# An attention, channel MLP and expert attention kernel: one operand's copies on another queue, early sums read out by another engine, and a new table of tile modes

## The chip, the cores and the metric

The kernel runs on one core of a Trainium2 chip. The metric is the device time of one execution in microseconds (us), a median over runs. The core has five instruction streams: TensorE (PE; its weight loads are shown apart as PEld), VectorE (DVE), ScalarE (ACT), GpSimd (POOL) and SyncE (SP), which here only issues transfers. Each stream runs its instructions in order; semaphores tie them together. Sums of TensorE stand in PSUM, everything else in SBUF.

## The reference

Three blocks follow one another on arrays of 2 batches, 768 positions and 512 columns. The first is an attention of 8 heads of width 64, in which a query sees only keys whose six projection signs equal its own; the second is a position mixer of rank 32 with a channel MLP; the third is four causal attentions, of which each position takes the best two by a gate.

```python
# 1: per head, S = 768, D = 64
mask = bucket(q @ proj)[:, None] == bucket(k @ proj)[None, :]
attn = softmax(where(mask, q @ k.T / 8, -1e9)) @ v
# 2: x is attn with the heads side by side (512 columns)
u = x + (x.T @ U @ V).T
x = u + relu(u @ w_ch1) @ w_ch2          # 512 -> 2048 -> 512
# 3: four experts, causal, width 64, best two by the gate
out = sum(gate_e * softmax(causal(x @ wq_e @ (x @ wk_e).T / 8)) @ (x @ wv_e) @ wo_e)
```

## The kernel before

The results need more than half precision, so nearly every operand is held as a high and a low half in float16, and a product takes two or three matmuls (high with high, high with low, low with high).

**First block (a1).** The work is 8 pairs of heads, four to a batch: (0,0) to (0,3), then (1,0) to (1,3). A head has 6 tiles of 128 queries by 768 keys, so a pair has 12 tiles and the block 96. For a tile TensorE makes the scores `sc` (L621, L626), VectorE reduces them (`L632`, which also moves them to SBUF as P32), ScalarE takes the exponent (L543 or L591). What follows goes by the tile's mode, from the table `A1_MODES`, which is run through again and again over a pair's 12 tiles. A mode of two letters names who makes the high half (L545 on ScalarE for A, L547 on VectorE for V) and who subtracts it to get the low half (L551, on GpSimd for P or VectorE for V); both halves are then turned by a transfer (`dma_start_transpose`, L643), and 18 matmuls of 64 columns (L555 to L557) multiply them with the values. A mode that begins with F keeps float32: TensorE transposes (L597), ScalarE or VectorE reads the result out (L602, L604, by the mode's second and third letter), and float32 matmuls (L606) multiply with the values, without a transfer.

**Operands of a pair** (`a1_prep`) are made one pair ahead. The queries' high half HQ lies in a staging tile TQ and goes by transfer into AQ and a second time into BQ (L454); so do the keys' halves into AK and BK (L461 to L463). The program's names carry buffer numbers; BQ and BK have two buffers, used by turns. The first pair has a path of its own (`a1_first`), in which `BQE1` makes the second copy.

**Weights.** The MLP's two matrices arrive as 64-bit floats, in 32 units of 128 by 512 words. A unit is a transfer into w or wx (L277), three integer operations on VectorE (L189, L192, L195) that make float32, a copy to float16 on ScalarE (L280) and a scaling and a subtraction on GpSimd (L281, L282). When units are asked for is set by counts: NWA0 over the first PRE0 tiles, NWA and NW1 over the next ones, and then NWB plus WRATE per step of the MLP (`need`).

**MLP.** Six tiles of the first product are summed early, over the first two quarters of the columns (`early`, L322), and moved by `EVICT` to the tiles acc. The first 512 positions go through `mlp_wide`: ph (L748, twelve matmuls of 512 columns a tile) is read out by L755 on ScalarE and L756 on VectorE, and px (L770) by L773 on VectorE. The other blocks go through `mlp_stream` (ph L806, px L824). `merge` weaves a1 and the MLP together by costs: MIX says how many a1 tiles are spread over how much MLP.

**Order.** The order above is only a wish. A list scheduler with a timeline of its own places each engine's instructions by priority (the order of writing, shifted by `sooner`, `AHEAD` and the like) and by when it expects operands and buffers to be free. So a changed count or mode moves instructions elsewhere too.

Of the kernel before, what the change touches and what calls it, by code (L numbers as in the profile page):

```python
# [15 lines left out]
AF = mybir.ActivationFunctionType  # L16
# [6 lines left out]
def kernel(  # L23
# [17 lines left out]
    nc = tc.nc  # L41
# [19 lines left out]
    CLIP = 8e9  # L61
    WPOOL = True
    A1_MODES = (
        [('AP', 'FAA'), ('FAV', 'AP', 'FAV'), ('AP', 'VP', 'FAV', 'AP', 'VP', 'AP', 'FAV', 'AP', 'VP', 'AP', 'FAV', 'FAV'), ('AP', 'FAA', 'VP', 'FAV')],
        [('AP', 'VP'), ('AP', 'AP', 'AV'), ('AP', 'AV', 'VP'), ('AP', 'AP', 'AV')],
    )
    A2_MODES = ("AP", "AP")
    MIX = (24, 2.2)
    LAST_MODES = ("PV", "AP", "PV", "T")
    VPOS = 1  # L70
    FPOS = 3
    BQE1 = lambda o, i: nc.scalar.activation(o, i, AF.Copy)
    KLE = nc.gpsimd
    KLE0 = (nc.vector, nc.gpsimd)
    SKE = lambda o, k, a: nc.scalar.activation(o, k, AF.Copy, scale=-0.125)
# [8 lines left out]
    PJ = nc.vector  # L84
    AHEAD = 80
    AHEAD2 = 150
    AHEAD3 = 300
    N4 = 7
    W4 = 1.0
    SOON = 20  # L90
# [3 lines left out]
    FIRST = 2  # L94
    SSE = lambda s: nc.scalar.activation(s, s, AF.Copy, bias=0.25e-9, scale=0.25)
    PRE1 = 48
    PRE0 = 42
    EVICT = nc.vector.tensor_copy
    XNB = 1
    LAGS = (2, 4, 4)  # L100
    LAST_LAGS = (1, 1, 1)
# [102 lines left out]
    VV = cp.tile([4 * R, S], FH, name="VV")  # L204
# [205 lines left out]
    HALF = (slice(0, D), slice(D, P))  # L410
# [19 lines left out]
    def q_halves(j, qn, AQ, BQ):  # L430
# [3 lines left out]
        nc.vector.scalar_tensor_tensor(lo, hi, 8.0, qn, op0=ALU.mult, op1=ALU.add)  # L434
        BQE1(BQ[HALF[0], j], hi)

# [6 lines left out]
    def a1_prep(b, p, wait):  # L443
        qn, kn, vn = nats.pop((b, p))
        n = f"{b}_{p}"
        AQ, AK, BQ, BK, V = a1_operands(b, p)
        TQ = sp.tile([P, 2, S], FH, tag="TQ", name=f"TQ_{n}")
        HQ, LQ = TQ[:, 0], TQ[:, 1]
        nc.scalar.activation(HQ, qn, AF.Copy, scale=-0.125)
        nc.vector.scalar_tensor_tensor(LQ, HQ, 8.0, qn, op0=ALU.mult, op1=ALU.add)  # L450
        for j, o in enumerate(HALF):
            nc.sync.dma_start(AQ[HALF[0], j], HQ[o])
            nc.sync.dma_start(AQ[HALF[1], j], LQ[o])
            nc.sync.dma_start(BQ[HALF[0], j], HQ[o])  # L454
        TK = sp.tile([P, 3, S], FH, tag="TK", name=f"TK_{n}")
        HK, SK, LK = TK[:, 0], TK[:, 1], TK[:, 2]
        nc.scalar.activation(HK, kn, AF.Copy)
# [676 lines left out]
    def merge(*a):  # L1134
        drain(merged(*a))
# [46 lines left out]
                yield from a2_stream(b, s0 // P, (s0 + n) // P)  # L1182

    NWA0 = 8
    NWA = 5
    NW1 = 16
    NWB = 18
    WRATE = 0.8

# [36 lines left out]

    merge(take(a1, PRE0), PRE0 * CA, w_stream(NWA0), NWA0)
    C = (PRE1 - PRE0) * CA
    merge(take(a1, PRE1 - PRE0), C, merged(w_stream(NWA), NWA - NWA0, early_stream(), NPRE), NPRE + NWA - NWA0)
    merge(take(a1, PH1 - PRE1), (PH1 - PRE1) * CA, w_stream(NW1), NW1 - NWA)  # L1230
    C = MIX[1] * UNIT
    merge(take(a1, MIX[0]), CA * MIX[0], part(mlp, C), C)
    C = LEAD[0] * UNIT
    merge(a1, CA * (NA1 - PH1 - MIX[0]), part(mlp, C), C)
    C = LEAD[1] * UNIT
# [13 lines left out]
    merge(take(g4, N4), N4, part(mlp, C), C)  # L1249
    ahead[0] = AHEAD3  # L1250
    drain(mlp)
# [59 lines left out]
```

## Time and profile before

| | |
|---|---|
| median of 3 runs | 606.88 us (603.32 to 608.47) |
| profiled execution, its own time | 604.46 us |
| span of its instructions | 602.7 us |
| mean granted TensorE clock | 0.984 |

The span is what the profile's rows cover; about 1.8 us of the execution's time lies outside it. A busy TensorE in a row is not TensorE at its peak: the end of a matmul is modelled, so matmuls that follow one another with gaps may still fill their stretch. The pace of matmuls that are packed shows in the chain of work, where each is counted from its start to the next one's start. In the names of rows a number at the end of a tile's name is left out (P is P32, x_0_0 an MLP sum).

### The profile page before, as it was taken

To read this page: it belongs to the slowest core of one execution; us is meant where nothing else is said; L and a number is where in the kernel's file an instruction comes from. 1 tells how busy PE (TensorE), PEld (TensorE's weight loads), DVE (VectorE), ACT (ScalarE), POOL (GpSimd) and SP (SyncE) were. 2 spreads that over 40 slices of the span, in tenths; PEclk is the share of its full clock that TensorE was granted. 3 is DMA by queue.
4 is the path that set the end of the run, shared out by engine and by line. 5 is a ranking of instruction groups with operands and counts; after the bars stand their busy time and mean duration, and the time that the engine had idled before them with its cause. 6 is when DMAs were issued, how large, how long until landed. Compare 5 with 4: busy or idle time off the path is not lost.

```text
span 602.7 us, 14989 instructions
## 1 busy us (share of the span) xinstructions
PE 555.8 (92%) x5982; PEld 416.1 (69%) x5982; DVE 412.1 (68%) x948; ACT 351.9 (58%) x753; POOL 260.3 (43%) x239
## 2 busy tenths in 40 slices
PE   3789996899899999799999989999999998999995
PEld 1468864776555545447888866878877898999754
DVE  6976897759999999858768455553564335455584
ACT  6798787767564665645768534672465216144683
POOL 6644579745967698622246400250134002002350
PEclk9889999999899999999999999999999999999998
DMA  8789899989999999782479910153046002004655
GB/s 268 170 174 179 225 209 263 187 216 216 316 190 208 237 216 240 159 197 63 92 133 141 177 25 10 36 94 92 4 86 125 36 1 46 12 18 41 121 106 114
DMA packets 176566, 82.00 MB, mean 136 GB/s; under 512 B 160368, under 2 KB 167152, under 8 KB 176496
## 3 DMA queue, kind: packets, MB, share of 16 engines
q1 hardware_dynamic: 176496, 81.04, 62.2%
q8 instruction: 47, 0.77, 0.6%
q14 instruction: 23, 0.19, 0.1%
HBM read 29.30 MB, written 3.15 MB: 54 GB/s over the span
## 4 chain that ended last, share of the span: by engine, by line
PE 59%; DVE 16%; DMA 11%; issue 5%; ACT 5%; POOL 2%; SPq 1%; DVEq 0%; ACTq 0%; POOLq 0%
PE px L824 12%; PE ph L806 11%; DMA PT<-HL 6%; PE px L770 3%; PE po L606 3%; DVE P L632 2%; PE pk L875 2%; PE pq L875 2%; PE sc L621 2%; PE sc L626 2%; PE pv L903 2%; PE ph L748 2%; PE pz L1106 2%; PE s L974 2%; DMA wx<-in_moe_w_ch_dram 2%
## 5 line engine op out<-in xcount | busy, mean ns | idle before, releaser
L551 POOL TENSOR_TENSOR HL<-P,HL 128x768 f16<-128x768 f32 (+5 forms) x91 | 121.3, 1338 | 258.4 <-ACT HL L545 197.2
L543 ACT ACTIVATE P<-P,m 128x768 f32<-128x768 f32 (+5 forms) x110 | 89.4, 813 | 40.7 <-DVE P L632 26.2
L806 PE MATMUL ph<-U,W 128*128 128x256 f16 (+1 forms) x960 | 95.4, 251 | 0.5 <-DVE hT L808 0.5
L824 PE MATMUL px<-hT,W 128*128 128x256 f16 (+1 forms) x960 | 94.1, 251 | 0.0
L824 PEld LDWEIGHTS <-W 128*128 128x128 f16 x960 | 78.2, 98 | 8.4
L806 PEld LDWEIGHTS <-W 128*128 128x128 f16 x960 | 77.0, 98 | 8.7 <-issue 0.8
L632 DVE TENSOR_SCALAR_CACHE_REDUCE P<-sc 128x768 f32<-128x768 f32 x80 | 74.9, 947 | 11.0 <-PE sc L626 10.9
L545 ACT ACTIVATE HL<-P 128x768 f16<-128x768 f32 (+5 forms) x91 | 63.1, 696 | 9.7 <-DMA PT<-HL 8.5
L555 PEld LDWEIGHTS <-PT 128*128 128x128 f16 x522 | 47.6, 98 | 16.8 <-DMA PT<-HL 8.3
L621 PE MATMUL sc<-AK,AQ 128*128 128x512 f16 x192 | 49.0, 335 | 6.2 <-DVE P L632 2.7
L556 PEld LDWEIGHTS <-PT 128*128 128x128 f16 x522 | 47.4, 98 | 5.4 <-issue 1.9
L555 PE MATMUL po<-V,PT 128*128 128x64 f16 x378 | 43.5, 193 | 6.6 <-DMA PT<-HL 3.2
L626 PE MATMUL sc<-BK,BQ 96*128 96x512 f16 x192 | 49.6, 336 | 0.0
L557 PEld LDWEIGHTS <-PT 128*128 128x128 f16 x522 | 47.5, 98 | 1.7 <-issue 0.2
L770 PE MATMUL px<-hT,W 128*128 128x512 f16 x192 | 44.4, 379 | 0.8 <-DVE acc L754 0.4
L808 DVE SCALAR_TENSOR_TENSOR hT<-ph,hT 128x256 f16<-128x256 f32 (+1 forms) x80 | 28.8, 366 | 23.1 <-ACT hT L807 22.3
L557 PE MATMUL po<-V,PT 128*128 128x64 f16 x378 | 44.2, 193 | 0.0
L556 PE MATMUL po<-V,PT 128*128 128x64 f16 x378 | 44.2, 193 | 0.0
L807 ACT ACTIVATE hT<-ph 128x256 f16<-128x256 f32 (+1 forms) x80 | 26.4, 334 | 28.9 <-PE ph L806 28.0
L748 PE MATMUL ph<-U,W 128*128 128x512 f16 x156 | 36.3, 380 | 1.7 <-DVE hT L756 1.3
L982 DVE TENSOR_SCALAR_CACHE_REDUCE P<-s 128x128 f32<-128x128 f32 (+5 forms) x48 | 29.3, 620 | 9.1 <-PE s L979 8.0
L770 PEld LDWEIGHTS <-W 128*128 128x128 f16 x192 | 18.1, 98 | 20.6 <-DVE acc L754 0.8
(257 smaller groups left out, 1252.1 us busy)
## 6 DMA issues: line engine op xcount, KB each, us to landing
w<-in_moe_w_ch_dram SPq DMA_DIRECT2D x17, 512.0 KB, 5.1
wx<-in_moe_w_ch_dram SPq DMA_DIRECT2D x15, 512.0 KB, 5.6
vn<-in_v_dram SPq DMA_DIRECT2D x8, 384.0 KB, 4.5
out_dram<-o SPq DMA_DIRECT2D x12, 256.0 KB, 2.1
kn<-in_k_dram SPq DMA_DIRECT2D x7, 384.0 KB, 4.6
qn<-in_q_dram SPq DMA_DIRECT2D x7, 384.0 KB, 4.0
AK<-TK SPq DMA_DIRECT2D x28, 96.0 KB, 2.7
AQ<-TQ SPq DMA_DIRECT2D x28, 96.0 KB, 3.1
```

The source lines that it names most:

```text
L543: nc.scalar.activation(P32, P32, AF.Exp, bias=m, scale=-1.0, accum_out=ssum)
L545: nc.scalar.activation(HL[:, 0], P32, AF.Copy)
L551: eng.tensor_tensor(HL[:, 1], P32, HL[:, 0], op=ALU.subtract)
L555: nc.tensor.matmul(o, PT[:, t, :], vh(t), start=(t == 0), stop=False)
L556: nc.tensor.matmul(o, PT[:, t, :], vl(t), start=False, stop=False)
L557: nc.tensor.matmul(o, PT[:, nk + t, :], vh(t), start=False, stop=(t == nk - 1))
L621: nc.tensor.matmul(ps[:, c0 : c0 + cn], aq[:, P * t : P * (t + 1)], ak[:, c0 : c0 + cn], start=True, stop=False,)
L626: nc.tensor.matmul(ps[:, c0 : c0 + cn], bq[:, P * t : P * (t + 1)], bk[:, c0 : c0 + cn], start=False, stop=True,)
L632: nc.vector.tensor_scalar(P32, ps[:, 0:S], CLIP, None, op0=ALU.min, op1=ALU.min, accum_out=m)
L770: nc.tensor.matmul(po, w, u, start=(i == 0), stop=(i == len(ops) - 1))
L806: nc.tensor.matmul(ph, w, u, start=(i == 0), stop=(i == len(ops) - 1))
L824: nc.tensor.matmul(po, w, u, start=(i == 0), stop=(i == len(ops) - 1))
```

## The change

It does five things. (1) HQ's second copies for pairs 2 to 8 (L454, 14 transfers of 64 by 768) are issued by ScalarE instead of SyncE; in the first pair the second copy, made by two ScalarE copies (L72), becomes two transfers on SyncE (L435). (2) The six early sums are read out by ScalarE (L98) instead of VectorE (L323). (3) Counts: PRE0 42 to 44, NWA 5 to 6, NW1 16 to 9, so that by the order of writing fewer weight units are asked for ahead of the MLP. (4) Modes: pair (0,3) goes from 3 AP, 3 VP, 6 F to 3 AP, 1 AV, 1 VV, 7 F. Of batch 1's 48 tiles, those that subtract on VectorE (AV) go from 12 to 2, AP from 26 to 35, VP from 10 to 11: pair (1,0) from 6 AP, 6 VP to 8 and 4; (1,1) from 8 AP, 4 AV to 12 AP; (1,2) from 4 AP, 4 AV, 4 VP to 9 AP, 3 VP; (1,3) from 8 AP, 4 AV to 6 AP, 4 VP, 2 AV. (5) MIX from 24 to 26 tiles, and AHEAD3 from 300 to 200.

```diff
--- before.py
+++ after.py
@@ -61,15 +61,15 @@
     CLIP = 8e9
     WPOOL = True
     A1_MODES = (
-        [('AP', 'FAA'), ('FAV', 'AP', 'FAV'), ('AP', 'VP', 'FAV', 'AP', 'VP', 'AP', 'FAV', 'AP', 'VP', 'AP', 'FAV', 'FAV'), ('AP', 'FAA', 'VP', 'FAV')],
-        [('AP', 'VP'), ('AP', 'AP', 'AV'), ('AP', 'AV', 'VP'), ('AP', 'AP', 'AV')],
+        [('AP', 'FAA'), ('FAV', 'AP', 'FAV'), ('AP', 'VP', 'FAV', 'AP', 'VP', 'AP', 'FAV', 'AP', 'VP', 'AP', 'FAV', 'FAV'), ('AV', 'FAV', 'FAV', 'AP', 'VV', 'FAA', 'FAA', 'FAV', 'AP', 'FAV', 'AP', 'FAV')],
+        [('VP', 'AP', 'VP', 'AP', 'VP', 'AP', 'AP', 'AP', 'VP', 'AP', 'AP', 'AP'), ('AP',), ('AP', 'VP', 'AP', 'AP'), ('AP', 'VP', 'VP', 'AV', 'AP', 'AP')],
     )
     A2_MODES = ("AP", "AP")
-    MIX = (24, 2.2)
+    MIX = (26, 2.2)
     LAST_MODES = ("PV", "AP", "PV", "T")
     VPOS = 1
     FPOS = 3
-    BQE1 = lambda o, i: nc.scalar.activation(o, i, AF.Copy)
+    BQE1 = nc.sync.dma_start
     KLE = nc.gpsimd
     KLE0 = (nc.vector, nc.gpsimd)
     SKE = lambda o, k, a: nc.scalar.activation(o, k, AF.Copy, scale=-0.125)
@@ -84,7 +84,7 @@
     PJ = nc.vector
     AHEAD = 80
     AHEAD2 = 150
-    AHEAD3 = 300
+    AHEAD3 = 200
     N4 = 7
     W4 = 1.0
     SOON = 20
@@ -94,8 +94,8 @@
     FIRST = 2
     SSE = lambda s: nc.scalar.activation(s, s, AF.Copy, bias=0.25e-9, scale=0.25)
     PRE1 = 48
-    PRE0 = 42
-    EVICT = nc.vector.tensor_copy
+    PRE0 = 44
+    EVICT = lambda o, i: nc.scalar.activation(o, i, AF.Copy)
     XNB = 1
     LAGS = (2, 4, 4)
     LAST_LAGS = (1, 1, 1)
@@ -451,7 +451,7 @@
         for j, o in enumerate(HALF):
             nc.sync.dma_start(AQ[HALF[0], j], HQ[o])
             nc.sync.dma_start(AQ[HALF[1], j], LQ[o])
-            nc.sync.dma_start(BQ[HALF[0], j], HQ[o])
+            nc.scalar.dma_start(BQ[HALF[0], j], HQ[o])
         TK = sp.tile([P, 3, S], FH, tag="TK", name=f"TK_{n}")
         HK, SK, LK = TK[:, 0], TK[:, 1], TK[:, 2]
         nc.scalar.activation(HK, kn, AF.Copy)
@@ -1182,8 +1182,8 @@
                 yield from a2_stream(b, s0 // P, (s0 + n) // P)
 
     NWA0 = 8
-    NWA = 5
-    NW1 = 16
+    NWA = 6
+    NW1 = 9
     NWB = 18
     WRATE = 0.8
```

The scheduler then moves much. The first place is VectorE in the second head of pair (1,1); the first list is before, the second now (w are weight units, U and xn the mixer's, x_0_0 and hT the MLP's).

```order
L632 TENSOR_SCALAR P_1_1_1_2_3525,m_1_1_2_3524<-sc_1_1_2_3519 128x768
L189 TENSOR_SCALAR w_14_x<-w_14_64_3061 128x512
L192 SCALAR_TENSOR_TENSOR w_14_x<-w_14_64_3061,w_14_x 128x512
L195 SCALAR_TENSOR_TENSOR w_14_32_3062<-w_14_64_3061,w_14_x 128x512
L551 TENSOR_TENSOR HL_1_1_2_3527<-P_1_1_1_2_3525,HL_1_1_2_3527 128x768
L189 TENSOR_SCALAR w_15_x<-w_15_64_3125 128x512
L652 TENSOR_TENSOR xn_1_3018<-po_1_0_3019,r_1_0_3405 128x6x64
L632 TENSOR_SCALAR P_1_1_1_3_3582,m_1_1_3_3581<-sc_1_1_3_3576 128x768
L192 SCALAR_TENSOR_TENSOR w_15_x<-w_15_64_3125,w_15_x 128x512
L208 SCALAR_TENSOR_TENSOR U_1_3119<-up_0_3608,U_0_3118 128x768
L195 SCALAR_TENSOR_TENSOR w_15_32_3126<-w_15_64_3125,w_15_x 128x512
L632 TENSOR_SCALAR P_1_1_1_4_3657,m_1_1_4_3656<-sc_1_1_4_3651 128x768
```

In the changed kernel the same place reads:

```order
L632 TENSOR_SCALAR P_1_1_1_2_3497,m_1_1_2_3496<-sc_1_1_2_3491 128x768
L208 SCALAR_TENSOR_TENSOR knw<-wqs,qnw 128x1024
L773 SCALAR_TENSOR_TENSOR x_0_0_2293<-px_0_2_0_3224,x_0_0_2293 128x512
L632 TENSOR_SCALAR P_1_1_1_3_3544,m_1_1_3_3543<-sc_1_1_3_3538 128x768
L652 TENSOR_TENSOR xn_1_2998<-po_1_0_2999,r_1_0_3378 128x6x64
L756 SCALAR_TENSOR_TENSOR hT_0_2292<-ph_0_3_0_3421,hT_0_2292 128x512
L773 SCALAR_TENSOR_TENSOR x_0_0_2293<-px_0_2_3_3369,x_0_0_2293 128x512
L756 SCALAR_TENSOR_TENSOR hT_0_2292<-ph_0_3_1_3468,hT_0_2292 128x512
L632 TENSOR_SCALAR P_1_1_1_4_3617,m_1_1_4_3616<-sc_1_1_4_3611 128x768
L208 SCALAR_TENSOR_TENSOR U_1_3088<-up_0_3570,U_0_3087 128x768
L756 SCALAR_TENSOR_TENSOR hT_0_2292<-ph_0_3_2_3483,hT_0_2292 128x512
L632 TENSOR_SCALAR P_1_1_1_5_3674,m_1_1_5_3673<-sc_1_1_5_3668 128x768
```

Before, weight units and a subtraction L551 stand between the reductions L632; now the units are through, and MLP read-outs (L756, L773) stand there.

The second place is ScalarE in the second head of the first pair, before and then now; BQ_128 is the buffer that this pair still reads, and TQ_2 the staging tile of pair (0,2).

```order
L545 ACTIVATE HL_0_1_2_548<-P_0_0_1_2_546 128x768
L214 ACTIVATE VV<-vf_403 128x384
L543 ACTIVATE P_0_0_1_4_604,ss_0_1_461<-P_0_0_1_4_604,m_0_1_4_603 128x768
L602 ACTIVATE PT_0_1_1_500<-tp_0_1_1_0_501 128x384
L602 ACTIVATE PT_0_1_1_500<-tp_0_1_1_1_506 128x384
L591 ACTIVATE P_0_0_1_5_645,ss_0_1_461<-P_0_0_1_5_645,m_0_1_5_644 128x768
L214 ACTIVATE VV<-vf_415 128x384
```

The same place now:

```order
L545 ACTIVATE HL_0_1_2_548<-P_0_0_1_2_546 128x768
L602 ACTIVATE PT_0_1_1_500<-tp_0_1_1_0_501 128x384
L214 ACTIVATE VV<-vf_415 128x384
L602 ACTIVATE PT_0_1_1_500<-tp_0_1_1_1_506 128x384
L454 DMA BQ_128<-TQ_2_671 64x768
L543 ACTIVATE P_0_0_1_4_604,ss_0_1_461<-P_0_0_1_4_604,m_0_1_4_603 128x768
L602 ACTIVATE PT_0_1_3_581<-tp_0_1_3_0_582 128x384
L591 ACTIVATE P_0_0_1_5_635,ss_0_1_461<-P_0_0_1_5_635,m_0_1_5_634 128x768
```

A transfer into BQ now stands among the exponents; it waits until TensorE has read that buffer for the last time in this pair.

Counted over the whole order: weight units through VectorE (L195, which also counts three units of U and V) ahead of the first reduction of pair (1,0) go from 12 to 15, with the lower counts of (3); MLP matmuls of 512 columns between the first scores of (1,1) and of (1,2) go from 168 to 225, and between those of (1,2) and (1,3) from 84 to 27 (there also 210 of 256 columns before, 196 now). Between the first scores of (1,0) and of (1,1) stand 96 of 512 columns in both, with 24 early ones before and 30 now. From the third part of px_0_512 on (of the MLP's second block), just ahead of the row at 350.21 us of the profile, TensorE's order is the same to the end of the program.

## Rows read from the trace of the kernel before

**Rows 1.** The page: busy time of each engine.
```profile
PE 555.8 (92%) x5982; PEld 416.1 (69%) x5982; DVE 412.1 (68%) x948; ACT 351.9 (58%) x753; POOL 260.3 (43%) x239
```

**Rows 2.** Windows: length, busy us and count of PE, PEld, DVE, ACT, POOL; clock, DMA.
```profile
15.80:44.80 29.00, 24.06 (x188) 15.57 (x189) 24.78 (x47) 25.02 (x50) 17.41 (x14) 0.87 0.78 168
44.80:76.90 32.10, 32.10 (x344) 27.23 (x342) 24.55 (x48) 24.87 (x48) 17.19 (x15) 0.96 0.94 210
76.90:107.80 30.90, 23.63 (x275) 17.67 (x273) 26.38 (x50) 24.03 (x46) 26.75 (x21) 1.00 1.03 228
107.80:141.80 34.00, 32.45 (x357) 25.58 (x355) 23.91 (x47) 23.59 (x48) 17.22 (x13) 1.00 0.89 217
141.80:196.90 55.10, 51.23 (x457) 29.42 (x456) 52.84 (x94) 32.63 (x60) 42.49 (x37) 0.97 1.00 226
196.90:254.40 57.50, 52.22 (x448) 28.01 (x448) 53.23 (x89) 36.90 (x64) 45.71 (x41) 1.00 0.93 213
254.40:312.90 58.50, 58.49 (x589) 41.69 (x588) 41.43 (x77) 32.12 (x62) 16.93 (x12) 1.00 0.56 119
312.90:350.20 37.30, 35.87 (x517) 30.38 (x514) 23.05 (x48) 24.52 (x47) 17.94 (x12) 1.00 0.93 158
```

**Rows 3.** The chain that ended last: start us, length us, what.
```profile
210.12 1.96 DVE HL L551
...
244.13 6.22 DMA PT<-HL
...
350.21 2.59 PE pk L875 x12
```

**Rows 4.** Groups by line, VectorE, 141.8 to 254.4 us: busy, mean ns, idle before.
```profile
L189 DVE TENSOR_SCALAR w_x<-w 128x512 uint32<-128x512 uint32 x12 | 8.3, 688 | 0.1
...
L551 DVE TENSOR_TENSOR HL<-P,HL 128x768 f16<-128x768 f32 x3 | 5.0, 1673 | 0.3 <-ACT HL L545 0.2
...
L547 DVE CAST HL<-P 128x768 f16<-128x768 f32 x6 | 5.0, 832 | 0.0
...
L773 DVE SCALAR_TENSOR_TENSOR x<-px,x 128x512 f32<-128x512 f32 x7 | 4.8, 683 | 2.8 <-PE px L770 2.8
...
L323 DVE COPY acc<-pe 128x512 f32<-128x512 f32 x4 | 2.7, 674 | 0.0
```

**Rows 5.** The chain: TensorE at full pace.
```profile
40.02 0.03 PE po L555
...
251.10 2.59 PE px L770 x12
...
253.69 0.33 PE sc L621 x2
...
275.04 1.31 PE ph L806 x12
```

**Rows 6.** The chain: TensorE in a tile of the F modes.
```profile
111.94 0.66 PE tp L597 x6
...
113.12 1.37 PE po L606 x12
```

**Rows 7.** Groups by line, ScalarE, 141.8 to 254.4 us.
```profile
L755 ACT ACTIVATE hT<-ph 128x512 f16<-128x512 f32 x6 | 3.5, 576 | 0.0
```

**Rows 8.** Line L454 on its own: ns min/median/max, first and last start us.
```profile
L454 SPq DMA_DIRECT2D BQ<-TQ x14: 461/594/1062, 23.6 to 253.1; - x14
...
DMA to landing us min/median/max: 2.2/2.8/5.2
```

**Rows 9.** Waits of the transfer queue: us in total, times, longest.
```profile
SPq L452 <- PE sc L626: 7.9, 5, 2.8
```

**Rows 10.** Timeline of the start, ScalarE.
```profile
8.42 0.84 ACT L72 ACTIVATE BQ<-AQ 64x768 f16<-64x768 f16 x1
```

**Rows 11.** Groups by line: VectorE 312.9 to 350.2 us; GpSimd 196.9 to 254.4 us.
```profile
L551 DVE TENSOR_TENSOR HL<-P,HL 128x768 f16<-128x768 f32 x4 | 4.5, 1126 | 5.6 <-ACT HL L545 5.6
...
L551 POOL TENSOR_TENSOR HL<-P,HL 128x768 f16<-128x768 f32 x8 | 14.3, 1790 | 6.5 <-ACT HL L545 6.3
```


## Prediction

> **What bounds the kernel now.** I read the page first, then the busy times cut by pairs of heads, then the chain of work, then the groups of lines in the stretches that the change touches. On the page TensorE is busy 92% of the span, VectorE 68%, ScalarE 58%, GpSimd 43% [rows 1]. That average hides three regimes, which the cut by pairs shows (a stretch begins at the first reduction L632 of its pair). In batch 0's pairs no engine is full: pair (0,2) lasts 30.90 us, with VectorE busy 26.38, GpSimd 26.75 and TensorE 23.63. In (1,0) and (1,1), where weight units and the MLP join, VectorE is busy 52.84 of 55.10 and 53.23 of 57.50 us, that is 94 to 96%, and TensorE is idle for 3.87 and 5.28 us. In (1,2) TensorE is busy 58.49 of 58.50, and in (1,3) 35.87 of 37.30 [rows 2]. The chain agrees: at 210 us it runs through a VectorE subtraction of 1.96 us and at 244 through a landing of 6.22, and it reaches the third block at 350.21 [rows 3]. From there the order on TensorE is unchanged to the end. So the 252.5 us after it stay, and the whole question is when TensorE gets there.
>
> How full TensorE really is shows in its packed pace, not in its busy time: twelve MLP matmuls of 512 columns take 2.59 us (0.216 each), twelve of 256 columns 1.31 (0.109), two score matmuls (half a tile's) 0.33, a value matmul 0.03 [rows 5]. Pairs (1,0) to (1,2) hold 372 matmuls of 512 columns by the order, 348 of the MLP and 24 early ones (80.4 us), 210 of 256 columns (22.9), and 36 tiles at 0.66 + 18 x 0.03 = 1.20 (43.2). Sign and mixer steps I put at 8 us, an estimate from some 150 narrow matmuls at 0.03 to 0.11. That makes 154.5 us of work in 55.1 + 57.5 + 58.5 = 171.1. So there are at most 16.6 us to win there, all in the two pairs that VectorE bounds.
>
> **The change part by part.**
>
> Pair (1,0). VectorE loses the four early read-outs that fall here (4 x 0.674 = 2.7 us; the other two lie in (0,3)) and two high halves (2 x 0.832 = 1.7), and gains one read-out of a float32 transpose, which I put at 0.55: 3.8 us less [rows 4]. ScalarE takes six early read-outs, at 0.576 by its read-out of the same shape [rows 7], and two more high halves; it is busy 32.63 of 55.10 [rows 2], which hides them. The bounds are 0 and 3.8; since VectorE is at 96% I take most, 2.5.
>
> Pairs (1,1) and (1,2). Three weight units have moved ahead of this place (9 operations at 0.688 = 6.2 us), and three subtractions leave VectorE for GpSimd (3 x 1.673 = 5.0) [rows 4]. In their place come seven MLP read-outs (7 x 0.683 = 4.8). VectorE so needs 6.4 us less in (1,1), and TensorE gets 225 - 168 = 57 more matmuls there, 57 x 0.216 = 12.3 us. Exactly those are missing in (1,2), together with 14 of 256 columns (1.5 us) that slip into (1,3). Pair (1,2) is bound by TensorE, so it falls by the full 13.8 us. Pair (1,1) grows by as much of the 12.3 as its gaps don't take up. If TensorE ran in (1,0) to (1,2) at 98% of its packed pace, 154.5 + 1.3 for the early sums - 1.5 would take 157.4, which is 13.7 less than now; with the 2.5 of (1,0) taken off, 11.2. The lower bound is nothing: the feed of operands (transfers of 6.22 us [rows 3] behind GpSimd's subtractions) may keep the gaps as they are. GpSimd itself hardly gets more in (1,1): four subtractions at 1.79 [rows 11] come, three units go; it is busy 45.71 of 57.50 [rows 2]. I take 5.5 of the 11.2, the middle, since VectorE's relief there (6.4) is about half of what TensorE would have to fill.
>
> Pair (1,3). The 14 matmuls arrive, 14 x 0.109 = 1.5 us; TensorE is nearly full [rows 2], so +1.5.
>
> Pair (0,2). The weight units moved ahead land here: by the order four more VectorE operations, 4 x 0.69 = 2.8 us [rows 4], on top of 26.38 of 30.90, and one more unit on GpSimd, which has 26.75 [rows 2]. Bounds 0 and +2.8; both engines would pass 90%, so I take +2.
>
> Pair (0,3). One more tile in an F mode costs TensorE 0.66 + 1.37 in place of 18 x 0.03 [rows 5, 6], 1.5 us, while the early sums leave this pair in part. VectorE gets two subtractions and a further unit and loses two read-outs and two copies; GpSimd loses three subtractions. At 34.00 us no engine but TensorE (32.45) is near its limit [rows 2]. Bounds -2 and +2; I take +0.5.
>
> The transfers. SyncE is spared 14 issues at 0.594 us, 8.3 in all [rows 8]; it was no bound on average, and I give nothing for it. ScalarE issues them instead. What an issue costs there no row shows: the bounds are 0 and SyncE's 0.594 each plus any wait, two to a pair. Its idle time is 3.98 us in the first pair and 6.9 or more in the next ones [rows 2], so 1.2 is covered; queued behind it on ScalarE are the exponents of the next tiles, and for those VectorE's copies and the transfers wait. I take 0, and 0 to +6 for the range. At the start two copies of 0.84 [rows 10] leave ScalarE, and two transfers that take about 2.8 to land [rows 8] come; the tiles that read them begin only after sign steps on VectorE, so 0, bounds -1 and +1.
>
> AHEAD3 and the tail cost nothing, since the order there is the same.
>
> The sum is -2.5 - 5.5 + 1.5 + 2 + 0.5 = -4.0. The profiled execution took 604.46 us in all, 1.8 more than its span; 604.46 - 4.0 = 600.5. The median of the three runs, 606.88, lies 0.4% above that execution and the lowest run 0.2% below it, so by the median the ratio would be 0.9895 and by the profiled run 0.993. I hold 600.5 as a time and let the chances carry the difference.
>
> **A rule against the change.** In (1,0) and (1,1) a subtraction on VectorE takes 1.673 us, in (1,3), where GpSimd is busy 17.94 of 37.30 us instead of four fifths, 1.126 [rows 2, 4, 11].
>
> The Trainium skill, page "SBUF — State Buffer", section "Who interferes with whom", says that a VectorE instruction with two SBUF inputs contends with a GpSimd instruction that reads SBUF, through one port pair that is held for the whole instruction, the later one waiting. By that rule a subtraction given to GpSimd would not leave VectorE alone: the two rows of 1.673 and 1.126 agree with such blocking, though the trace doesn't show who held what. By it the time would be that of the second rival below, 606.0; without it the sum stands.
>
> **The rivals.**
>
> Full relief: TensorE reaches its packed pace in all of (1,0) to (1,2), and the early pairs hide their additions. 604.46 - 13.7 + 1.5 = 592.3. For it: (1,2) runs full now. Against: in (1,0) the same nine weight units still have to pass VectorE before the MLP's quarters can start. Chance 0.17.
>
> No net gain: GpSimd, with four subtractions more in (1,1), holds VectorE up. 4 x 1.79 = 7.2 us of held time against 6.4 of relief leaves (1,1) and (1,2) where they are; with -2.5 from (1,0) and the +4.0 of the others the sum is +1.5, 606.0. For it: the slow subtractions above. Against: as many GpSimd operations leave with the three units. Chance 0.23.
>
> Slower: ScalarE held by a transfer. L454 on ScalarE waits until TensorE has read the buffer for the last time and until an older transfer has landed; on SyncE such waits for scores come to 7.9 us over 5 times, up to 2.8 [rows 9]. Each such hold stops the exponents behind it. It decides from the point where a hold outlasts ScalarE's slack, about 2 us per transfer in the first pair (3.98 over two). At 2.8 plus 0.594 for an issue, eight transfers in batch 0 hold it 27 us; what passes beyond 2 us each, 8 x 1.4 = 11, is lost. 600.5 + 11 = 611.5. Against: by the order the second transfer of a pair stands next to the exponent of the last tile that reads the buffer, which needs the same scores. Chance 0.12.
>
> That the change doesn't do what it says holds for one part in any case: with lower counts more weight units, not fewer, come ahead. Its price is the +2 in (0,2) and part of the gain in (1,1).
>
> **How the numbers follow.** The forecast, a gain of 1 to 8 us, has 0.48, and the rivals 0.17, 0.23 and 0.12. The predicted time is the forecast's, 600.5. The range goes from 592, full relief, to 609, the no-gain case by the median of the runs with its additions; this leaves out most of the slow case and little else. Against the median of 606.88, 1% lies at 600.8, so a little over half of the forecast's mass and all of full relief count as faster by over 1%: 0.43. Within 1%, about what a measurement of this kernel can tell from no change: 0.45. Slower by over 1%: 0.12.
>
> **What would show it.** Right: in the profile after, pair (1,1) lasts longer than before or about as long and (1,2) some 13 us less; no L551 on VectorE in (1,1); VectorE's busy share there falls below 90% while TensorE's idle time shrinks; the third block (L875) starts near 346 us, and its distance to the end is unchanged. Wrong: (1,0) as long as before with VectorE at 95% (no relief); waits of ScalarE's queue for scores (L454) of over 2 us (held); pair (0,2) longer by over 3 us. What I can't see is how the many small moves in batch 0's pairs add up; if they cost or give more than 3 us, the forecast fails there.

## The result, and the profile after

The changed kernel takes 611.57 us (median of 13 runs, 609.95 to 618.47) against 605.24 for the kernel before, measured beside it on the same chip: 1.0108 times as long, with a 95% interval of 1.0082 to 1.0135. Forecast were 600.5 us and a range of 592 to 609. It is slower by 1.1%, and the range missed it. Ratios leave disturbed executions out, so they can differ a little from the quotient of two medians.

The page of the profile after; its counts answer to [rows 1]:

```profile
PE 563.0 (93%) x5982; PEld 417.7 (69%) x5982; DVE 411.5 (68%) x935; ACT 354.0 (58%) x757; POOL 273.6 (45%) x246
```

Windows of the changed kernel, cut like [rows 2] at the first reduction of each pair; the last row is the stretch from L875 to the end (length; busy us and count of PE, PEld, DVE, ACT, POOL; clock; DMA):

```profile
15.80:46.20 30.40, 26.24 (x217) 17.61 (x218) 27.14 (x48) 23.85 (x48) 16.28 (x13) 1.00 0.90 207
46.20:77.50 31.30, 28.89 (x298) 23.22 (x296) 25.15 (x50) 25.81 (x51) 19.39 (x15) 1.00 1.05 230
77.50:109.80 32.30, 27.07 (x287) 20.00 (x288) 29.95 (x55) 24.18 (x46) 26.75 (x22) 0.89 0.98 204
109.80:142.90 33.10, 31.73 (x345) 25.61 (x344) 26.98 (x49) 25.25 (x51) 17.85 (x14) 1.00 0.95 225
142.90:201.50 58.60, 52.30 (x473) 29.55 (x471) 50.38 (x89) 37.30 (x67) 43.38 (x37) 1.00 0.99 220
201.50:269.40 67.90, 66.21 (x515) 34.71 (x512) 49.46 (x86) 37.94 (x66) 46.03 (x39) 1.00 0.84 181
269.40:317.70 48.30, 47.60 (x505) 35.67 (x504) 35.45 (x63) 29.25 (x57) 21.18 (x14) 1.00 0.58 109
317.70:357.20 39.50, 37.98 (x538) 32.27 (x537) 24.77 (x48) 23.03 (x43) 23.36 (x16) 1.00 0.94 151
357.20:608.20 251.00, 238.45 (x2811) 197.50 (x2807) 132.06 (x441) 117.70 (x319) 49.07 (x51) 1.00 0.29 57
```

Read against [rows 2], L875 starts 7.0 us later and the tail keeps its length (251.0 for 252.5), as was forecast of the tail. Batch 0 grows by 1.1 us (127.1 for 126.0), pair (1,0) by 3.5, (1,1) and (1,2) together by 0.2, (1,3) by 2.2. Subtracting TensorE's busy time from each length and adding up the eight pairs gives its idle time: 24.4 us before, 23.4 now. Its busy time went from 310.1 to 318.0. So VectorE is relieved (50.38 of 58.60 us in (1,0), 49.46 of 67.90 in (1,1), 86 and 73% where it was 96 and 93), and yet TensorE waits about as long as before and works 8 us longer.

Where about half of those 8 us go shows in the timeline of TensorE in pair (1,2). In the kernel before the sixteen sign matmuls of pair (1,3) (L477, 32 output columns each, a group's four going to four different column ranges) stand together:

```profile
287.12 0.39 PE L477 MATMUL sg<-AQ,PQ 128*32 128x512 f16 x2
287.13 0.39 PE L477 MATMUL sg<-AK,PK 128*32 128x512 f16 x2
287.35 0.38 PE L477 MATMUL sg<-AQ,PL 128*32 128x512 f16 x2
287.66 0.39 PE L477 MATMUL sg<-BK,PB 64*32 64x512 f16 x2
```

In the changed kernel the same step begins at 288.40 and ends at 296.06:

```profile
288.40 0.39 PE L477 MATMUL sg<-AQ,PQ 128*32 128x512 f16 x1
288.72 0.20 PE L557 MATMUL po<-V,PT 128*128 128x64 f16 x1
288.85 0.39 PE L477 MATMUL sg<-AQ,PQ 128*32 128x512 f16 x1
289.17 0.20 PE L555 MATMUL po<-V,PT 128*128 128x64 f16 x1
...
291.03 1.47 PE L806 MATMUL ph<-U,W 128*128 128x256 f16 x12
292.44 0.39 PE L477 MATMUL sg<-BK,PB 64*32 64x512 f16 x1
...
295.78 0.28 PE L477 MATMUL sg<-BK,PB 64*32 64x256 f16 x1
295.99 0.20 PE L557 MATMUL po<-V,PT 128*128 128x64 f16 x1
```

The starts tell most. Together, four sign matmuls begin within 0.01 us and all sixteen take 1.47 us (287.12 to 288.59). Apart, with one value matmul of 64 columns between each two, a sign matmul and its neighbour take 0.45 us (288.40 to 288.85; 0.35 with 256 columns). The step lasts 7.66 us, of which 1.41 are a tile of the MLP in its midst (291.03 to 292.44). So 6.25 us go to what takes 1.47 + 15 x 0.03 = 1.9 in the other order: 4.3 us lost, while TensorE shows as busy throughout.

Running one behind the other instead of side by side is the smaller part of that. By an estimate from the packed pace of [rows 5], sixteen sign matmuls in a row and the 15 value matmuls would take 8 x 0.216 + 8 x 0.109 + 15 x 0.03 = 3.05 us, 1.1 more than 1.9. The other 3.2 us lie in the changes from one kind to the other, some 0.1 us each: the value matmul begins 0.32 us after a sign matmul of 512 columns (288.40 to 288.72), where 0.216 is the pace, and the next sign matmul 0.13 after the value matmul (288.72 to 288.85), where 0.03 is. What TensorE does in that time isn't in the trace.

Three more stretches of the profile after bear on the forecast. In (1,0) two operations of VectorE wait, and its queue with them:

```profile
162.89 0.69 DVE L189 TENSOR_SCALAR w_x<-wx 128x512 uint32<-128x512 uint32 x1 [2.94 <-DMA wx<-in_moe_w_ch_dram]
...
197.90 0.96 DVE L450 SCALAR_TENSOR_TENSOR TQ<-TQ,qn 128x768 f16<-128x768 f16 x1 [2.02 <-ACT TQ L449]
```

The chain (start us, length us, what) leads into the first of them through GpSimd and then a load; the reduction behind it in VectorE's queue starts at 163.62, and it is 20.7 us after the pair's first one, where before it was 17.0:

```profile
143.27 5.53 DMA AQ<-TQ
...
156.80 0.63 POOL wx L281
...
157.95 4.91 DMA wx<-in_moe_w_ch_dram
...
163.62 0.96 DVE P L632
```

In (1,1) the chain runs on GpSimd with no pause over 0.1 us from 214.42 to 232.79 us, through fifteen operations, and ends in a landing:

```profile
214.42 1.65 POOL HL L551
216.07 1.12 POOL W L282
...
231.16 1.61 POOL HL L551
232.79 5.90 DMA PT<-HL
```

The waits of SyncE's queue tell the same (us in total, times, longest). Its transposes waited 15.8 us, 14 times, for this line before; now:

```profile
SPq L643 <- POOL HL L551: 36.9, 18, 4.9
```

The moved transfers, on ScalarE's queue (ns min/median/max, then the time to landing), take 471 ns an issue where SyncE's took 594 [rows 8], and land in 4.2 us (median), where it was 2.8:

```profile
L454 ACTq DMA_DIRECT2D BQ<-TQ x14: 468/471/502, 16.9 to 261.2; - x14
...
DMA to landing us min/median/max: 2.6/4.2/7.6
```

They hardly hold ScalarE up. The longest hold is the last one, in ScalarE's timeline: its work ends at 259.57, the transfer is issued at 261.20, as soon as the scores that read the buffer are through, and the exponent behind it would have had to wait in any case, until VectorE's reduction was done:

```profile
258.97 0.60 ACT L755 ACTIVATE hT<-ph 128x512 f16<-128x512 f32 x1
261.20 0.47 ACTq L454 DMA_DIRECT2D BQ<-TQ  x1
262.29 0.94 ACT L543 ACTIVATE P<-P,m 128x768 f32<-128x768 f32 x1 [2.72 <-DVE P L632]
```

### The profile page after: what moved, and what is told of

Same layout as the page of the kernel before. It is cut to its first block, busy times and chain, and to the rows that moved or that the text cites. A ratio compares the mean times of both kernels' runs of the same rounds, so it can differ in the third digit from the quotient of the medians.

```text
span 608.2 us, 14990 instructions
## 1 busy us (share of the span) xinstructions
PE 563.0 (93%) x5982; PEld 417.7 (69%) x5982; DVE 411.5 (68%) x935; ACT 354.0 (58%) x757; POOL 273.6 (45%) x246
## 4 chain that ended last, share of the span: by engine, by line
PE 56%; DMA 14%; DVE 12%; POOL 7%; ACT 6%; issue 4%; SPq 1%; DVEq 0%; POOLq 0%; ACTq 0%
PE px L824 12%; PE ph L806 11%; DMA PT<-HL 8%; PE px L770 4%; POOL HL L551 3%; PE po L606 3%; PE pq L875 2%; PE ph L748 2%; PE pk L875 2%; PE sc L621 2%; PE sc L626 2%; PE pv L903 2%; DMA PT<-more_X 2%; PE pz L1106 2%; ACT P L543 2%
## 5 line engine op out<-in xcount | busy, mean ns | idle before, releaser
L551 POOL TENSOR_TENSOR HL<-P,HL 128x768 f16<-128x768 f32 (+5 forms) x100 | 135.8, 1364 | 262.9 <-ACT HL L545 227.3
L806 PE MATMUL ph<-U,W 128*128 128x256 f16 (+1 forms) x960 | 97.1, 251 | 0.2 <-DVE hT L808 0.2
L632 DVE TENSOR_SCALAR_CACHE_REDUCE P<-sc 128x768 f32<-128x768 f32 x80 | 75.6, 948 | 9.3 <-PE sc L626 8.6
L621 PE MATMUL sc<-AK,AQ 128*128 128x512 f16 x192 | 51.4, 345 | 7.9 <-DVE more_X L632 4.7
L555 PE MATMUL po<-V,PT 128*128 128x64 f16 x372 | 46.0, 193 | 10.3 <-DMA PT<-HL 8.1
L626 PE MATMUL sc<-BK,BQ 96*128 96x512 f16 x192 | 51.6, 345 | 0.0
L770 PE MATMUL px<-hT,W 128*128 128x512 f16 x192 | 46.2, 379 | 1.5 <-DVE hT L756 0.6
L557 PE MATMUL po<-V,PT 128*128 128x64 f16 x372 | 46.7, 193 | 0.0
L556 PE MATMUL po<-V,PT 128*128 128x64 f16 x372 | 46.2, 193 | 0.0
```

The lines of the kernel that those rows point to most:

```text
L551: eng.tensor_tensor(HL[:, 1], P32, HL[:, 0], op=ALU.subtract)
L555: nc.tensor.matmul(o, PT[:, t, :], vh(t), start=(t == 0), stop=False)
L556: nc.tensor.matmul(o, PT[:, t, :], vl(t), start=False, stop=False)
L557: nc.tensor.matmul(o, PT[:, nk + t, :], vh(t), start=False, stop=(t == nk - 1))
L621: nc.tensor.matmul(ps[:, c0 : c0 + cn], aq[:, P * t : P * (t + 1)], ak[:, c0 : c0 + cn], start=True, stop=False,)
L626: nc.tensor.matmul(ps[:, c0 : c0 + cn], bq[:, P * t : P * (t + 1)], bk[:, c0 : c0 + cn], start=False, stop=True,)
```

## The experiments

Twelve kernels hold the signs together or apart, or do or undo one or two parts of the change; six only redraw the order. The signs were the first suspect.

**The signs, both ways.** `sooner(n, f)` raises the priority of what f writes by n.

```diff
-        later(wait, signs)
+        later(wait, lambda: sooner(200 if (b, p) == (1, 3) else 0, signs))
```

> The changed kernel with one edit: the 16 sign matmuls of pair (1,3) (L477) get a priority 200 higher, so that they stand one behind the other again; in the changed kernel each of the 16 stood between two value matmuls, and the step from 288.40 to 296.06 us held one F-free tile of the MLP (1.47 us) and some 6.2 us of alternation, where the same 16 took 1.47 us in the kernel before. Theory A (alternating matmuls of 32 and of 128 output columns cannot overlap, and pair (1,2) is bound by TensorE): the step falls back to 1.5 us and the time from 611.6 to about 607 (606 to 608.5); pair (1,2) shortens by 4 to 5 us and the read-out L875 comes as much earlier. Theory B (the stretch has slack, some other engine or a transfer is late next): the step shortens but the time stays within 1 us of 611.6.

Measured: 1.0029 (1.0003 to 1.0056), 606.76 us. Against the changed kernel's 1.0108 that is 0.8%, or 4.8 us. In the profile the step takes 1.46 us (286.64 to 288.10), and (1,2) falls from 48.3 to 43.8:

```profile
201.60:269.50 67.90, 66.14 (x508) 34.62 (x508) 49.70 (x86) 37.94 (x66) 46.16 (x39) 1.00 0.85 182
269.50:313.30 43.80, 43.12 (x505) 33.67 (x504) 33.75 (x63) 28.89 (x57) 21.19 (x14) 1.00 0.63 120
```

In the kernel before, the reverse (`sooner(-40 ...)`), which hardly moves the other engines (4 rows of difference on VectorE, 2 on ScalarE, none on GpSimd and SyncE; up to the step in (1,2) the order is that of the kernel before on every engine):

> The kernel before with one edit: the sign matmuls of pair (1,3) get a priority 40 lower, and the scheduler then places each of the 16 between two value matmuls, as in the changed kernel; all else in the order is nearly the same. Theory A: the step grows from 1.5 to some 6 to 8 us and the time by 3.5 to 5 us, from 605.2 to 609 to 610. Theory B: the time stays within 1 us of 605.2, since in the kernel before other engines have the last word in pair (1,2).

Measured: 1.0074 (1.0044 to 1.0103), 609.3 us, which is 4.5 us. The step lasts from 290.98 to 299.32, and (1,2), which was 58.5 long, shows:

```profile
258.40:321.20 62.80, 62.80 (x590) 43.54 (x588) 41.54 (x77) 32.02 (x62) 16.24 (x11) 1.00 0.51 105
```

Theory A holds in both directions and B falls. The step's price is 4.3 us in the pair and 4.5 to 4.8 in the time.

e2 also shows how far the profile of one execution can be trusted. With the order of the kernel before, pair (0,2) lasts 33.3 us at a granted clock of 0.85, where [rows 2] have 30.90 at 1.00, and pair (1,0) 57.2 us with TensorE idle for 6.1, where they have 55.10 and 3.87. So 2 us in the length of one pair need no change of the kernel.

**Batch 1's modes.** e3 is the changed kernel with the old table for batch 1, e4 the kernel before with the new one.

```diff
-        [('VP', 'AP', 'VP', 'AP', 'VP', 'AP', 'AP', 'AP', 'VP', 'AP', 'AP', 'AP'), ('AP',), ('AP', 'VP', 'AP', 'AP'), ('AP', 'VP', 'VP', 'AV', 'AP', 'AP')],
+        [('AP', 'VP'), ('AP', 'AP', 'AV'), ('AP', 'AV', 'VP'), ('AP', 'AP', 'AV')],
```

> The changed kernel with batch 1's modes as they were (all else changed). By the forecast's steps VectorE has 10 subtractions more in its way again and is the late one in pairs (1,0) to (1,2): these grow by 3 to 8 us, the time goes to 614 to 619. By the rival (GpSimd, with the subtractions that VectorE gave away, holds up the transposes): it gets 12 subtractions less, (1,1) and (1,2) together shorten by up to 4 us, 607 to 612. The sign matmuls of (1,3) stand apart here too, so that cost stays in.

> The kernel before with batch 1's new modes alone. By the forecast's steps (VectorE relieved in (1,0), (1,1) and (1,2)): 4 to 8 us off, 597 to 601. By the rival (GpSimd takes over as the late engine): within 2 us of 605. The sign matmuls of (1,3) stand in three groups here, so nearly together.

Measured: e3 1.0158 (1.0108 to 1.0208), e4 1.0038 (1.0015 to 1.0060). The new modes cost the kernel before 0.4%, where the forecast's steps gave it a gain of 4 to 8 us. In the changed kernel they seem worth 0.5%, but the intervals of e3 and the changed kernel overlap. Pairs (1,0) to (1,2) grow from 174.8 to 176.9 us in e3, less than the 3 to 8 that the forecast's steps gave. Pair (1,0) of e3, and then (1,0) of e4:

```profile
141.00:191.40 50.40, 45.87 (x405) 26.24 (x404) 43.67 (x76) 31.52 (x58) 37.65 (x29) 0.97 1.00 217
```

```profile
142.70:200.50 57.80, 50.69 (x461) 28.57 (x459) 53.66 (x94) 33.76 (x62) 45.42 (x37) 1.00 1.02 227
```

TensorE is idle for 4.5 us with the old modes and 7.1 with the new; in the kernels they were made from it was 6.3 (e3's) and 3.9 (e4's). The new modes of (1,0) are nowhere seen to go with less waiting; that they go with more isn't shown, since e2 has 6.1 with the order of the kernel before.

**Parts undone in e1.** All four keep the signs together.

```diff
 e5: nc.scalar.dma_start(BQ[HALF[0], j], HQ[o])  ->  nc.sync.dma_start(...); BQE1 -> two ScalarE copies
 e6: EVICT = lambda o, i: nc.scalar.activation(...)  ->  nc.vector.tensor_copy
 e7: MIX 26, PRE0 44, NWA 6, NW1 9  ->  24, 42, 5, 16
 e8: A1_MODES of (1,1): ('AP',)  ->  ('AP', 'AP', 'AV')
```

> The changed kernel with its signs together (606.8 us, the kernel that this one is held against), and HQ's second copies back where they were: on SyncE for pairs 2 to 8, two ScalarE copies in the first pair. By the forecast (the move to ScalarE's queue costs nothing): within 1.5 us of 606.8. By the rival that ScalarE is held by them: 2 to 5 us less. By the opposite (SyncE's queue is late before pair (1,0), and gets two transfers a pair more): 1 to 3 us more, with the stretch between the third and the fourth reduction of pair (1,0) (11.0 us in the kernel before, 15.9 with the signs together) longer.

Measured: 1.0067 (1.0028 to 1.0107). The interval overlaps that of e1. The middle, 2.3 us above e1, lies in the last theory's range, but the third to fourth reduction took 13.8 us, not longer than 15.9, so its mechanism isn't there. ScalarE's hold would have shown as a gain; there is none.

> The changed kernel with its signs together and the six early sums read out by VectorE again. By the forecast's step (VectorE is the late engine ahead of and in pair (1,0), and lost 3.8 us of work there): 2 to 3 us more than 606.8. By a theory C (the stretch between the third and fourth reduction of (1,0) grew from 11.0 to 15.9 us because ScalarE has six read-outs of 0.58 us more among the copies of the weights and of the next pair's operands): that stretch falls to 11 to 13 us, the time by 2 to 4 us.

Measured: 1.0039 (0.9993 to 1.0086), no difference from e1 that can be seen, and that stretch still took 15.2 us, so theory C's mechanism falls. Pair (1,0) lasts 57.2 us, as in e1 (57.1). The interval is too wide to exclude the forecast's 2 to 3 us by the time alone.

> The changed kernel with its signs together and the old counts (MIX 24, PRE0 42, NWA 5, NW1 16). By the forecast (the new counts put three weight units ahead of pair (1,0) and cost 2 us in (0,2)): 1 to 3 us less than 606.8. In this kernel's order the old counts put yet more units ahead of (1,1) (20 through VectorE where 18 were; the count of the kernel before is 16), so a theory D (units ahead of the MLP are what lengthens batch 0 and (1,0)) gives 1 to 3 us more.

Measured: 1.0148 (1.0065 to 1.0232), 1.2% above e1; by the middle of its wide interval that is more than any theory's price. Pair (0,2) takes 38.5 us and (1,0) 61.5. The direction is that of theory D.

> The changed kernel with its signs together and pair (1,1) alone in its old modes (four subtractions from GpSimd back to VectorE). By the forecast's step (VectorE is the late engine in (1,1)): (1,1) and (1,2) together grow by 3 to 5 us from 111.7, 609.5 to 611.5. By the rival (GpSimd, which ran without a break from 214 to 233 us in (1,1), is the late one): they shorten by 1 to 4 us, 603 to 606.

Measured: 1.0044 (1.0008 to 1.0080); (1,1) and (1,2) together 112.5 for 111.7 us. Four subtractions moved back cost 0.8 us in the pairs: neither the forecast's 3 to 5 nor the rival's gain.

**Pair (0,3)'s modes, alone and with the early read-outs,** on e1:

```diff
 e9:  A1_MODES of (0,3): the 12 new ones  ->  ('AP', 'FAA', 'VP', 'FAV')
 e10: the same, and EVICT -> nc.vector.tensor_copy
```

> The changed kernel with its signs together (1.003 times the kernel before) and pair (0,3) in its old modes: one F tile less. Theory E (TensorE at its packed pace fills most of the stretches from (0,3) on, so its work counts in full): the F tile's 1.5 us comes off, ratio 0.999 to 1.002. The forecast booked 0.5 us for it: ratio 1.002. A rival (three high halves more are turned by transfers at the end of batch 0, and SyncE's queue is what (1,0) waits for): 1.004 to 1.008.

> As the run before, and the early sums read out by VectorE again. By the forecast (VectorE is late in (1,0), and these 6 read-outs of 0.68 us count there): 2 to 3 us more than the run before. By theory E (VectorE's work has cover there): within 1 us of it.

Measured: 1.0028 (0.9993 to 1.0063), which tells none of the three apart, and 1.0067 (1.0030 to 1.0104). The F tile's work leaves (0,3) (31.1 us for 32.2), but it comes back in (1,0), 60.2 us for 57.1. The step between the two, 0.4%, is what the forecast gives the early read-outs; e6 showed 0.1% for the same edit, and both differences are within their intervals, so what the read-outs cost stays open.

**Single parts put into the kernel before,** signs of (1,3) together:

```diff
 e11: MIX 24, PRE0 42, NWA 5, NW1 16  ->  26, 44, 6, 9
 e12: L454 on nc.scalar, BQE1 = nc.sync.dma_start
```

> The kernel before with the new counts alone (MIX, PRE0, NWA, NW1), its signs of (1,3) held together by priority, without which these counts alone set them apart. By the forecast's step of 2 us for weight units moved ahead: ratio 1.002 to 1.005. By a theory that the counts are what shortens TensorE's idle time in (1,1) and (1,2) (9.1 us before, 7.1 with the changed kernel's signs together): 0.994 to 0.998.

> The kernel before with HQ's second copies by transfers as in the changed kernel (ScalarE's queue; SyncE in the first pair), signs of (1,3) held together. By the forecast (the move costs and gives nothing): ratio 0.998 to 1.002. By the mirror of the run that undid it and came out 0.4% slower: 0.994 to 0.998. By the rival that ScalarE is held: 1.005 to 1.012.

Measured: 1.0128 (1.0087 to 1.0169) and 1.0172 (1.0122 to 1.0221). No theory had these sizes: the 1.0172 lies above even the range of the rival that ScalarE is held, and that rival's mechanism is not in the trace. Waits of e12 between 76 and 120 us:

```profile
DVE more_X L632 <- POOL xs L670: 4.9, 1, 4.9
...
PE up L691 <- DVE T L215: 4.2, 1, 4.2
```

The transfers' own line takes 0.469 us an issue at the median, as in the changed kernel. What is late is a reduction that waits for GpSimd, and then the mixer. In e11 the chain shows, in pair (0,2), a single transpose that took 10.77 us to land; what held it was not followed:

```profile
93.71 10.77 DMA PT<-more_X
```

Each of these two parts alone costs more than a per cent, at places of its own, and undoing the counts costs as well (e7). That suggested that the price is the new order as such.

**Redraws.** Six kernels hold the instructions of the kernel before (r1, r2, r5) or of the changed one (r3, r4, r6), signs of (1,3) together; only a weight of the list is turned, so that the scheduler places them anew:

```diff
 r1, r3: AHEAD = 80  ->  90
 r2, r4: CA = 2700  ->  2750
 r5, r6: CA = 2700  ->  2650
```

> The kernel before, signs of (1,3) together, with AHEAD (the head start that the priorities of a1 get over the MLP) 90 for 80: same instructions, another order. Theory F (the order as such is worth as much as the parts; the kernel before is a good draw of many): 0.3 to 1.5% slower, with TensorE idle at new places in (1,0) to (1,2). Theory G (the order costs nothing by itself; what the parts cost is their own work and waits): within 0.3% of the kernel before.

> The kernel before, signs of (1,3) together, with CA (the cost that the weave books for an a1 tile) 2750 for 2700: same instructions, another order. Theory F: 0.3 to 1.5% slower. Theory G: within 0.3%.

> The changed kernel, signs of (1,3) together (1.003 times the kernel before), with AHEAD 90 for 80. Theory F: it goes either way by 0.3 to 1.5%, since this kernel is no better a draw than others. Theory G: 1.000 to 1.006.

> The changed kernel, signs of (1,3) together, with CA 2750 for 2700; in its order the signs of (1,1) stand together too (six groups in the changed kernel). Theory F: either way by 0.3 to 1.5%. Theory G: 1.000 to 1.006, or up to 0.3% less for the signs of (1,1).

> The kernel before, signs of (1,3) together, CA 2650 for 2700: same instructions, another order. Theory F (a redraw costs, and the kernel before is a good draw): 1.005 to 1.015, as the other two redraws (1.0133, 1.0113). Theory G (the order costs nothing by itself): 1.000 to 1.003.

> The changed kernel, signs of (1,3) together, CA 2650 for 2700. Theory F with parts that have no net effect: 1.005 to 1.015, level with the redraws of the kernel before. Theory F with the forecast's gain of 0.7% by the parts: 1.000 to 1.007, that much below them.

| edit | kernel before | changed kernel |
|---|---|---|
| none but the signs | 1 (as it is; its signs stand together) | 1.0029 (1.0003 to 1.0056) |
| AHEAD 90 | 1.0133 (1.0093 to 1.0173) | 1.0093 (1.0056 to 1.0131) |
| CA 2750 | 1.0113 (1.0069 to 1.0158) | 1.0102 (1.0065 to 1.0140) |
| CA 2650 | 1.0230 (1.0153 to 1.0307) | 1.0167 (1.0096 to 1.0239) |

The page of r1 has the counts of [rows 1] on every engine:

```profile
PE 555.8 (91%) x5982; PEld 413.8 (68%) x5982; DVE 413.8 (68%) x948; ACT 352.3 (58%) x753; POOL 260.4 (43%) x239
```

and TensorE's busy time is the same, yet its pair (1,0) lasts 60.20 us with 9.4 idle, where [rows 2] have 55.10 and 3.87 and e2 has 57.2 and 6.1:

```profile
141.50:201.70 60.20, 50.76 (x457) 28.72 (x454) 54.82 (x94) 33.28 (x61) 43.44 (x37) 0.97 0.95 221
```

Theory F holds: the same instructions in another order cost the kernel before 1.1 to 2.3%, and G is out. The kernel before is faster than all three redraws of itself, and the changed kernel with its signs together (e1) has the lowest ratio beside its three. Edit by edit the changed kernel's redraws lie 0.40, 0.11 and 0.63% below those of the kernel before, 0.4% or 2.3 us in the mean. None of the three differences stands clear of its intervals, and neither no gain by the parts nor the forecast's 0.7% is excluded by them. No version is shown to beat the kernel before. The redraws also carry the edit that holds the signs together; that edit alone was not run on the kernel before.

## Why the prediction was wrong

**The step that failed.** The sum left the order on TensorE out. It took the price of each moved step by itself and everything else as staying where it was. The sixteen sign matmuls of (1,3) stood in it as work of fixed length ("Sign and mixer steps I put at 8 us, an estimate from some 150 narrow matmuls"), the same before and after, so that setting them apart came in at nothing. e1 and e2 show that it costs 4.5 to 4.8 us. That is most of the measured 1.08% (6.5 us), and less than half of the 10.5 us between that and the forecast's -4.0. The rest, some 6 us, is what e1 misses the forecast by with its signs in place. It is of the size that a redraw of the order costs (0.6 to 2.3%, r1 to r6), and for that too the sum had no term. It saw a danger of small moves, but only in batch 0's pairs. Which placements make up the rest was followed in the traces for some stretches and not undone one by one, so its cause stays open. One of them is the same loss once more, and e1 keeps it: of the sign matmuls that stand in pair (1,1), five have a value matmul behind them in the changed kernel, one in the kernel before.

```profile
228.08 0.39 PE L477 MATMUL sg<-AQ,PQ 128*32 128x512 f16 x1
228.40 0.20 PE L556 MATMUL po<-V,PT 128*128 128x64 f16 x1
...
230.22 0.20 PE L557 MATMUL po<-V,PT 128*128 128x64 f16 x1
...
231.53 0.20 PE L555 MATMUL po<-V,PT 128*128 128x64 f16 x1
```

By an estimate from the starts that is 1.9 us lost where the kernel before loses 0.5. No run undoes it alone; r4, where that step stands together, moves much else.

**Pair (1,0): -2.5, came out +3.5.** The pair did not follow VectorE's relief: VectorE is busy for 2.5 us less there, and the pair is not shorter. Its 96% was read as a bound. Part of what fills it is weight units and read-outs, which a scheduler can also place elsewhere. That this is why the relief bought nothing is argued, not shown. What ends last in the changed kernel ahead of the fourth reduction is the feed: GpSimd's L281, then a load of 4.91 us, then VectorE's L189. From the third reduction to the fourth it takes 16.7 us, in e1 15.9 and in e8 16.0, where the order of the kernel before takes 11.0 and, in e2, 10.6. The length of the whole pair is less certain: the changed kernel, e1 and e8 share their order up to (1,1), and their (1,0) took 58.6, 57.1 and 57.6 us; the kernel before and e2 share theirs and took 55.1 and 57.2. So the miss is 2.4 to 6 us, not one number.

**Pairs (1,1) and (1,2): -5.5, came out +0.2.** The windows moved as was forecast: (1,1) grew (57.5 to 67.9), (1,2) shrank, no L551 is left on VectorE in (1,1), its share fell below 90%, and TensorE's idle time there went from 5.3 to 1.7 us. (1,2) did not fall by 13.8 but by 10.2, since the signs stood apart; in e1 it fell by 14.7 and the two together by 4.3, near the 5.5. That VectorE's relief did it is not shown: e8 gives VectorE its four subtractions back, and the two pairs grow by 0.8 us instead of 3 to 5; with the new modes alone (e4) they last 116.2 us, no less than before. So the nearness of 4.3 to 5.5 may be luck. The rival of a GpSimd that takes over was half right: GpSimd ran without a pause, and over the whole run the transposes waited for its subtractions 36.9 us instead of 15.8; but taking four subtractions off it again (e8) gave nothing.

The two rows behind that rival, 1.673 and 1.126 us for a subtraction on VectorE [rows 4, 11], are means of two kinds, and so are the 1.350 us of the two that are left in (1,3):

```profile
325.96 1.64 POOL L551 TENSOR_TENSOR HL<-P,HL 128x768 f16<-128x768 f32 x1 [0.49 <-DVE HL L547]
...
326.68 1.74 DVE L551 TENSOR_TENSOR HL<-P,HL 128x768 f16<-128x768 f32 x1
...
342.51 0.96 DVE L551 TENSOR_TENSOR HL<-P,HL 128x768 f16<-128x768 f32 x1 [1.97 <-ACT HL L545]
```

The one that begins beside a subtraction on GpSimd ends 0.82 us after GpSimd's, and the other, alone, takes 0.96 in all. Over the traces of all twenty kernels the 103 subtractions of this shape with no GpSimd operation beside them took 0.94 to 0.96 us; of the 81 beside one, 50 took over 1 us, up to 2.21. The rule named with that rival, of the Trainium skill's page "SBUF — State Buffer", section "Who interferes with whom", agrees with that: the later one waits. What failed in the rival is its price. It took the whole 7.2 us of GpSimd's added subtractions as held time, but with VectorE's own subtractions gone from (1,1) little there could be held: by an estimate, VectorE's operations in (1,1) run over the length that each kind has undisturbed by 0.4 us in all, where it was 2.2 in the kernel before.

**Pair (1,3): +1.5, came out +2.2.** Right in sign; TensorE is busy 37.98 us there for 35.87.

**(0,2) +2, (0,3) +0.5.** They came out at +1.4 and -0.9. TensorE was busy 27.07 us for 23.63 in (0,2) at a granted clock of 0.89, and e2 shows (0,2) 2.4 us longer at 0.85 with the order of the kernel before, so the +1.4 can't be put down to the weight units. In the profiles the granted clock of (0,2) is 1.00 in the kernel before alone and 0.82 to 0.95 in the other nineteen kernels, where it lasts 31.0 to 38.5 us; whether the lower clock or the waiting came first, and how much of the misses it makes up, isn't told apart. Batch 0 as a whole moved by 1.1 us, inside the 3 that the text allowed. Two readings there were wrong without bearing on the sum: TensorE is full in (0,1) (32.10 of 32.10 us), and VectorE's 53.23 of 57.50 us in (1,1) is 93%, not 94 [rows 2].

**The transfers: 0.** ScalarE is hardly held, as the trace after and e12's say. In the first pair the 0 was too low. The line of L435 alone, in the changed kernel:

```profile
L435 SPq DMA_DIRECT2D BQ<-AQ x2: 488/498/509, 6.8 to 10.9; - x2
...
DMA to landing us min/median/max: 5.3/5.4/5.5
```

The forecast put 2.8 for such a landing, and 5.4 it takes. The first pair lasts 29.7 to 32.0 us (median 30.1) in the twelve kernels that have these transfers, and 28.6 to 29.2 (median 28.6) in the eight that don't: 1.5 us, beyond the bound of 1. It isn't shown that the landings do it. The first reduction comes at 15.8 us before and after, and all twelve also issue L454 from ScalarE and have another order in that pair. What the other pairs of batch 0 do to it differs from kernel to kernel.

**The tail: 0.** It came out at -1.5 in the profile (251.0 for 252.5), with the order unchanged; e1's took 252.8. Right, with 1.5 us of difference between executions.

**No net gain, 606.0,** was the rival nearest to e1 (606.76) in number. Its mechanism isn't what happened, so that is luck; that the changed kernel went past it is the signs.

## What to carry to other kernels

Where a list scheduler or a planner sets the order, measure two or three redraws that change no work before pricing an edit: here they move the time by 1 to 2%, more than the whole change was forecast to be worth, and a kernel that is itself a lucky draw, as this one seems to be, can lose to edits that are sound by themselves. An engine that is 95% busy need not bound a stretch: relieved of 2.5 us, VectorE in (1,0) gave nothing back. Sum also what the engine that ends last waits for, and set that against the relief. Compare two executions of one order before reading 2 us out of one pair of a profile. Read the new order for narrow matmuls that ran side by side: one wider matmul between each two of them undoes it, and the engine still shows as busy.

## What the runs showed of the hardware

Sixteen matmuls of 32 output columns to four column ranges took 1.47 us together; with a matmul of 128 columns by 64 between each two they took 0.45 us per turn with 512 moving columns and 0.35 with 256, 6.25 us in all (some 0.1 us, by the estimate above, at each change from one kind to the other), and the whole kernel 0.74% (0.44 to 1.03) more for one such step. The durations that the trace gives to a sign matmul are the same in both orders (0.39 and 0.28 us); only the distance of the starts tells. The Trainium skill, page "TensorE: Matmul & The Clock Gate", section "The mechanism", says that matmuls start and end in program order and that those on different tiles of the array overlap; by that a full-width neighbour would end the overlap, and the starts in both traces agree. That alone comes to 1.1 of the 4.3 us lost.

A subtraction of 128 by 768 on VectorE took 0.94 to 0.96 us with no GpSimd operation beside it (103 of them) and up to 2.21 beside one.
